# Turning q and k of the second batch by DMA instead of by TensorE, in a fused attention and mixture kernel

## The chip, the cores and the metric

The kernel runs on one core of one Trainium2 chip. The metric is device time in microseconds of one execution. Five engines run their own instruction queues in order: TensorE (PE, with its weight loads shown as PEld), VectorE (DVE), ScalarE (ACT), GpSimd (POOL) and SyncE (SP). SP and POOL also issue DMA transfers, SP through the hardware-made queue (q1 in the profile) and POOL through the software-made one (q0). All transfers are carried by the same 16 DMA engines.

## What is computed

Attention over a sliding window of 128 positions plus 4 sink positions, for 4 batches, 8 heads, 768 positions and head size 64; its output, 3072 tokens of 512 values, then goes through a mixture of 4 experts, each of two matrix products with a ReLU between, summed by normalised weights.

```python
scores = scale * np.matmul(q, k.transpose(0, 1, 3, 2))
keep = is_sink | in_window
scores = np.where(keep, scores, -1000000000.0)
a = np.exp(scores - np.max(scores, axis=-1, keepdims=True))
attn = np.matmul(a / (np.sum(a, axis=-1, keepdims=True) + 1e-09), v)
...
p = domain_probs / (domain_probs.sum(-1, keepdims=True) + 1e-09)
for e in range(E):
    h = np.maximum(x @ w1[e], 0.0)
    out += p[:, e:e + 1] * (h @ w2[e])
```

## The kernel before

**Tiles.** A batch has 6 blocks of 128 positions (`tb`), taken as 3 groups of 256 (`g`), and 4 pairs of heads (`hp`). POOL loads q and k of a block as rows, cast to bf16, into a `qkn` buffer (`load_nat`, L188; there are six such buffers), and v into `vx` (`load_v`, L253). The scores need q and k with the head dimension on the partitions: that is `qkT`, of which there is one buffer, so a batch can be turned only when the scores of the batch before are done.

**Two ways to turn.** For batches 0 and 1, `transposes` (L502) lets TensorE turn four 128x128 pieces of one group and head pair into a PSUM bank (`tr`), and ACT or DVE copies the bank to `qkT` (`copy`, L226). For batches 2 and 3, `turn_nat` (L198) issues one DMA transpose of 128x1024 elements per block on SP (L202).

**Attention** of a group and head pair: scores (L619) into two banks, exponentials on ACT (`aT`, L644), masks on DVE (L638), values (`od`, L685, with the sinks' part at L678), a reciprocal on DVE (`R`, L712), four multiplications on ACT (`onat`, L724). When the four head pairs of a group are done, SP turns `onat` into `xT` by DMA (L702), the input of the mixture. The sink keys (L543) and sink matmuls (L580) come from `qkT` too.

**Mixture.** Batch 0 goes through plain products (`hps`, L1002; `acc`, L1305). Later batches partly use products with fewer multiplications (`cps`, L1080; `acc`, L1234), whose operands DVE forms (`T`, L1054, from `xT`). While batch 1's attention runs, the mixture of batch 0 fills TensorE; while batch 2's runs, that of batch 1, and so on.

**What sets the order.** The schedule is written out by a planner in the kernel itself. It keeps a clock for each engine (`t`), charges each step by small formulas (`pe`, `act`, `dve`, `pool`, `sp`, `lands`), and at each turn of the main loop (L1363) emits the step that its books call ready, attention steps being held back until they are due against the share of mixture work done. Every engine then executes its instructions in the emitted order, with semaphores for what it waits on. Six PSUM banks (`ring`) serve all steps but the accumulators.

**Around the change.** When batch 0's attention is emitted (L1369), the gates are worked out, the remaining weights are queued on POOL, and then the rows and v of batch 1. Batch 1's attention begins with 12 `flip` steps, each one call of `transposes`, spread among its other steps. The first flip of its last group queues the rows of batch 2 on POOL and puts their six turns on the list `turns` (L820). A turn is emitted from L1380: only when the planner has its rows landed, when the earlier batch has no scores left to emit, and when no second product of batch 0 is pending (`mix.second`). After the last turn of batch 2, POOL copies two elements of `qkT` into `held` (L1384); this makes POOL wait for the turn, and the row loads of batch 3 follow it.

Of the kernel before, what the change touches and what calls it, by code (L numbers as in the profile page):

```python
# [16 lines left out]
def kernel(  # L17
# [12 lines left out]
    nc = tc.nc  # L30

    B, H, S, D = q.shape
# [12 lines left out]
    NQB = S // P  # L45
    NHP = H // 2
# [6 lines left out]
    NG = S // G  # L53
# [7 lines left out]
    START = {0: 1, 1: 1, 2: 3, 3: 3}  # L61
# [2 lines left out]
    PAIR = 1  # L64
    BEHIND = 800
    CHORES = 3
    BIASED = 1
    FAST = tuple(START)
    UNITS = ("P1", "P5", "P6", "P2", "P7", "P3", "P4")
# [5 lines left out]
    t = {"pe": 1200.0, "act": 0.0, "dve": 0.0, "pool": 1280.0, "sp": 800.0, "sw": 6500.0, "hw": 0.0}  # L75
# [20 lines left out]
    def pool(cols, *deps, fixed=190):  # L96
        at = max([t["pool"], *deps])
        t["pool"] = at + fixed + cols * 1.8
        return t["pool"] + 35
# [57 lines left out]
    landed = {}  # L157
# [147 lines left out]
    def weight_form1(e):  # L305

        w = w1_sb[e].rearrange("p (k d) (m f) -> p m k d f", k=2, m=2)
        A11, A12, A21, A22 = w[:, 0, 0], w[:, 0, 1], w[:, 1, 0], w[:, 1, 1]
        if e not in forms1:
            if START[e] < B - 1:  # L310
                x = wpool.tile([P, 3, NDB // 2, F // 2], BF16, name=f"vf_{e}", tag=f"vf_{e}")
                x = [x[:, i] for i in range(3)]
            else:
                x = [sb.tile([P, 2, H, D], BF16, name="qkn", tag="qkn", bufs=NQB) for _ in range(3)]
                x = [i.rearrange("p d h c -> p d (h c)") for i in x]
            forms1[e] = {"P1": A11, "P2": A12, "P3": x[2], "P4": A22, "P5": x[0], "P6": x[1], "P7": A21}
            formed1[e] = 0
        x = forms1[e]
        if formed1[e] == 0:
            nc.vector.tensor_add(x["P5"], A21, A22)  # L320
        elif formed1[e] == 1:
            nc.vector.tensor_sub(x["P6"], x["P5"], A11)
        elif formed1[e] == 2:
            nc.vector.tensor_sub(x["P3"], A12, x["P6"])
        else:
            nc.vector.tensor_sub(A21, A11, A21)
        formed1[e] += 1
        forms1_at[e] = dve(1024, rate=1.92)
# [3 lines left out]

    def form1_due(e):
        n = formed1.get(e, 0)
        if START[e] == B - 1 and turned_at.get((B - 1, NQB - 1), 1e12) > t["pe"]:
            return False
        return landed.get(("w1", e), 1e12) < t["pe"] and (n < 3 or n == 3 and not left1[e])

# [225 lines left out]
            run("pool")  # L564

    def turned(b, g, *hps):
        if b < 2:
            return [turned_at.get((b, g, hp), 1e12) for hp in hps or range(NHP)]
        return [turned_at.get((b, tb), 1e12) for tb in range(2 * g + 2)]

# [188 lines left out]
    class Attention:  # L759


        def __init__(self, b):
            self.b = b
            self.flips = [("transposes", b, g, hp) for g in range(NG) for hp in range(NHP)] if b < 2 else []
            self.todo, self.scored, self.valued = [], [], []
            for g in range(NG):
                if g == (1 if b == 0 else 0):
                    self.todo.append(("keys", b, 0, 0))
                self.todo += [("scores", b, hp, g) for hp in range(NHP)]
                if g and (b < ONE or g == 1):  # L770
                    self.todo.insert(2 - NHP if b == 0 else -NHP, ("sinks", b, g, 1 if b < ONE else 2))
            self.total = len(self.todo) + len(self.flips) + (1 if b else 2) * NG * NHP
            self.steps = 0
# [32 lines left out]
        def emit(self, step):  # L806
            self.steps += 1
            if step == "turn":
                turn(*self.valued.pop(0))
            elif step == "values":  # L810
                u = self.scored.pop(0)
                values(*u)
                if u[0] == 0:
                    self.valued.append(u)
                elif u[1] == NHP - 1 and u[0] + 1 < B:
                    v_loads(u[0] + 1, u[2])
            elif step == "flip":
                _, b, g, hp = self.flips.pop(0)
                transposes(b, g, hp)
                if (b, g, hp) == (1, NG - 1, 0):  # L820
                    nat_loads(2, range(NQB))
                    turns.extend((2, tb) for tb in range(NQB))
            elif step == "two":
                self.steps += 1
                for i in range(2):
                    _, b, x, y = self.todo.pop(0)
                    scores(b, x, y, i)
                    self.scored.append((b, x, y))
            else:
                kind, b, x, y = self.todo.pop(0)  # L830
                if kind == "scores":
                    scores(b, x, y)
                    self.scored.append((b, x, y))
                elif kind == "sinks":
                    sinks(b, x, y)
                elif kind == "keys":
                    sink_keys(b)
                    sink_values(b)
# [506 lines left out]
    def nat_loads(b, tbs):  # L1345
        loads.extend((load_nat, b, tb) for tb in tbs)
# [16 lines left out]
    while mix.more() or att.more():  # L1363
        now = t["pe"]

        if not att.more() and ahead == B - 1 and not wide:
            wide = 1
            mix.widened()
        if not att.more() and not loaded:  # L1369
            loaded = 1  # L1370
            gates_by_row()
            loads += [(load_w1, 3), (load_w2, 3)]
            for tb in range(NQB):
                loads.append((load_nat, 1, tb))
                if tb % 2:
                    loads += [(load_v, 1, (tb - 1,)), (load_v, 1, (tb,))]
        if loads and t["pool"] < now + 1500 and load_ready(loads[0]) < now + 1500 and free_ring(loads[0]):
            x = loads.pop(0)
            x[0](*x[1:])
        if turns and not mix.second and landed.get(("qk", *turns[0]), 1e12) < now and (turns[0][0] <= ahead or turns[0][0] == ahead + 1 and not att.todo):  # L1380
            x = turns.pop(0)
            turn_nat(*x)
            if x == (2, NQB - 1):
                nc.gpsimd.tensor_copy(out=held, in_=qkT[2][:, 1, NHP - 1, S - 2:S])  # L1384
                pool(2, turned_at[2, NQB - 1])
                nat_loads(3, range(NQB))
                turns += [(3, tb) for tb in range(NQB)]
        flush(now)
        mix.tokens()
        mix.chore()  # L1390
        if ahead:
            next_form()
        if ahead + 1 < B and not att.more() and (ahead == 0 or (ahead + 1, 0) in turned_at) and (ahead == 0 or mix.done >= sum(work[:ahead])):
            ahead += 1
            att = Attention(ahead)
            upto = mix.done
        share = (sum(work[:ahead]) - upto) * 0.96
        due = ahead == 0 or att.steps * share <= (mix.done - upto) * att.total
        opts = []
        if att.more():  # L1400
            opts = [(max(r, now), (0 if due else 3) - 0.1 * (step == "two"), "att", step) for r, step in att.options()]
        s2, p = mix.second_ready(), mix.product_ready()
        behind = max(t["dve"] - now, 0.0) + 500 * sum(x[2] == "dve" and x[0] < now + 300 for x in pend)
        opts.append((max(p, now), 1 if behind > BEHIND else 2.5, "product", None))
        opts += [(max(f, now), 2, "first", x) for f, x in mix.firsts()]
        opts.append((max(s2, now), 1 if mix.since >= 1 else 2.5, "second", None))
        soonest = min(o[0] for o in opts)
        if soonest > now + 40 and flush(soonest, True):
            continue
        if soonest < 20000 and soonest > now + 220:  # L1410
            idle_products(acc[1], 1, G)
            continue
        if soonest > 1e11:
            if loads:
                x = loads.pop(0)
                x[0](*x[1:])
            else:
                turn_nat(*turns.pop(0))
            continue
        r, _, kind, step = min(opts, key=lambda o: (o[0] > now + 40, o[0] if o[0] > now + 40 else 0, o[1]))  # L1420
        assert r < 1e11
        if kind == "att":
            att.emit(step)
        elif kind == "first":
            mix.emit_first(step, r)
        elif kind == "product":
            mix.emit_product()
        else:
            mix.emit_second()
# [36 lines left out]
```

The softmax here doesn't subtract the row's maximum and nothing guards it: scores larger than these inputs give would overflow.

## Time and profile before

| | us |
|---|---|
| median of 4 runs | 372.28 (372.0 to 372.53) |
| the profiled execution | 372.0, of which the profile's span is 370.3 |

| group of instructions | count | mean ns | busy us |
|---|---|---|---|
| PE transposes, `tr` (L513) | 96 | 219 | 7.8 |
| ACT read-outs of 512 columns, `qkT` from `tr` (L226) | 14 | 594 | 7.7 |
| DVE read-outs of 512 columns, `qkT` from `tr` (L226) | 6 | 422 | 2.4 |
| SP issue of a DMA transpose of `qkn` (L202) | 12 | 1282 (median) | |
| ACT multiplications, `onat` (L724) | 144 | 325 | 33.3 |

The span is the profiled execution as its instruction records show it; the time of the run is somewhat longer. "Busy" of a group adds the durations with overlaps taken out. A matmul's duration is the time that it spends in TensorE's pipeline, and consecutive ones overlap, so the pace of a series is read from its start and the start of what follows. The software queue's packets took 51.8% of the 16 DMA engines' span, the hardware queue's 21.5%. The granted TensorE clock was 0.999.

### The profile page before, as it was taken

The page shows a single profiled execution, that of the slowest core. Times are in us where ns is not written, and L with a number is a line of the kernel's source. Part 1 is how long each engine was busy: PE and PEld are TensorE (multiplying, and loading weights), DVE is VectorE, ACT ScalarE, POOL GpSimd, SP SyncE. Part 2 cuts the span into 40 slices and gives each one's busy share as a digit, 9 for nine tenths or more (in the row PEclk, how much of TensorE's full clock was granted, in tenths as well). Part 3 has the DMA queues.
Part 4 walks back from the last instruction along what each step waited for, and adds up shares of the span by engine and source line. Part 5 has one row for each costly group of instructions (what it writes and reads, how often), then busy time and mean ns, then how long its engine had stood idle before and what let it go on. Part 6 is the DMA issues. An engine that isn't in the chain of part 4 may idle for free.

```text
span 370.3 us, 9961 instructions
## 1 busy us (share of the span) xinstructions
PE 361.0 (97%) x4167; PEld 299.5 (81%) x4167; DVE 287.2 (78%) x636; ACT 157.6 (43%) x402; POOL 71.3 (19%) x91
## 2 busy tenths in 40 slices
PE   6899999999999999999999999999999999999996
PEld 2585766667767788898888898899999999999985
DVE  5674997674554799779969979869898988899860
ACT  4764723685665245446435445552103213222110
POOL 8935113708040192010020000000000000000000
PEclk9999999999999999999999999999999999999999
DMA  9999999949999999519692041215002111020011
GB/s 164 165 189 198 210 212 180 155 30 107 150 126 206 166 120 112 74 57 88 113 165 81 13 104 30 44 44 87 16 19 84 30 43 58 16 73 2 2 58 57
DMA packets 110952, 35.63 MB, mean 96 GB/s; under 512 B 94276, under 2 KB 106404, under 8 KB 110908
## 3 DMA queue, kind: packets, MB, share of 16 engines
q0 software_dynamic: 77520, 17.31, 51.8%
q1 hardware_dynamic: 32332, 17.18, 21.5%
q8 instruction: 32, 0.52, 0.6%
q10 hardware_dynamic: 1056, 0.52, 0.5%
q14 instruction: 12, 0.10, 0.1%
HBM read 40.45 MB, written 6.34 MB: 126 GB/s over the span
## 4 chain that ended last, share of the span: by engine, by line
PE 87%; DVE 6%; DMA 3%; ACT 2%; issue 1%; ACTq 0%; DVEq 0%
PE acc L1234 29%; PE hps L1002 20%; PE cps L1080 19%; PE acc L1305 9%; PE sps L619 3%; PE od L685 2%; DMA xT<-onat 2%; DMA kraw<-in_k_dram 2%; PE tr L513 1%; ACT aT L644 1%; PE od L678 1%; DVE H L1026 1%; DVE aT L638 1%; DVE onat L715 1%; PE tx L743 1%
## 5 line engine op out<-in xcount | busy, mean ns | idle before, releaser
L1002 PE MATMUL hps<-xT,w 128*128 128x256 bf16 x768 | 95.6, 273 | 0.1
L1002 PEld LDWEIGHTS <-w 128*128 128x128 bf16 x768 | 72.3, 98 | 12.2 <-issue 2.6
L1234 PEld LDWEIGHTS <-H 128*128 128x128 bf16 x600 | 56.0, 98 | 6.4 <-issue 0.8
L644 ACT ACTIVATE aT<-sps 128x512 bf16<-128x512 f32 (+1 forms) x96 | 47.2, 571 | 30.6 <-PE sps L619 30.6
L1080 PEld LDWEIGHTS <-w 128*128 128x128 bf16 x768 | 48.2, 98 | 2.0 <-issue 0.5
L1234 PE MATMUL acc<-w,H 128*128 128x256 bf16 x360 | 48.0, 273 | 0.0
L724 ACT ACTIVATE onat<-od,R 128x64 bf16<-128x64 f32 x144 | 33.3, 325 | 34.0 <-DVE R L712 32.1
L1305 PE MATMUL acc<-w,H 128*128 128x512 bf16 x192 | 45.4, 379 | 0.0
L1099 DVE SCALAR_TENSOR_TENSOR H<-cps,gates 128x512 bf16<-128x512 f32 x57 | 38.7, 684 | 2.1 <-PE cps L1080 1.2
L1277 ACT COPY osb<-acc 128x256 f32<-128x256 f32 x36 | 13.5, 375 | 58.4 <-PE acc L1234 55.7
L1026 DVE SCALAR_TENSOR_TENSOR H<-hps,gates 128x512 bf16<-128x512 f32 x44 | 30.0, 686 | 9.3 <-PE hps L1002 9.1
L255 POOL DMA_DIRECT2D vx<-in_v_dram x24 | 21.3, 896 | 74.6 <-PE od L685 65.9
L1305 PEld LDWEIGHTS <-H 128*128 128x128 bf16 x192 | 18.3, 98 | 17.5
L1234 PE MATMUL acc<-wf,H 128*128 128x256 bf16 x240 | 31.9, 273 | 0.0
L1015 ACT ACTIVATE H<-hps 128x512 bf16<-128x512 f32 x36 | 21.5, 598 | 23.9 <-PE hps L1002 23.6
L1234 PEld LDWEIGHTS <-S 128*128 128x128 bf16 x288 | 27.0, 98 | 3.3 <-issue 0.5
L1080 PE MATMUL cps<-T,w 128*128 128x128 bf16 x384 | 29.3, 219 | 0.0
L1080 PE MATMUL cps<-xT,w 128*128 128x128 bf16 x384 | 29.1, 219 | 0.0
L1108 ACT COPY cps<-cps 128x512 f32<-128x512 f32 x24 | 13.8, 575 | 33.1 <-PE cps L1080 31.0
L1080 PEld LDWEIGHTS <-vf 128*128 128x128 bf16 x432 | 26.9, 98 | 1.0 <-issue 0.3
L1317 DVE SCALAR_TENSOR_TENSOR osb<-acc,scale_t,osb 128x512 f32<-128x512 f32 x18 | 13.5, 749 | 15.6 <-PE acc L1305 15.6
L190 POOL DMA_DIRECT2D qkn<-in_q_dram x22 | 19.8, 899 | 18.2 <-PE tr L513 9.0
(116 smaller groups left out, 532.3 us busy)
## 6 DMA issues: line engine op xcount, KB each, us to landing
w<-in_moe_w_dram POOLq DMA_DIRECT2D x7, 1024.0 KB, 18.9
out_dram<-osb SPq DMA_DIRECT2D x23, 256.0 KB
gates<-gate_rows SPq DMA_DIRECT2D x36, 128.0 KB
vx<-in_v_dram POOLq DMA_DIRECT2D x24, 128.0 KB, 6.4
qkn<-in_q_dram POOLq DMA_DIRECT2D x22, 128.0 KB, 6.8
qkn<-in_k_dram POOLq DMA_DIRECT2D x22, 128.0 KB, 7.0
w<-in_moe_w_dram POOLq DMA_DIRECT2D x2, 512.0 KB, 8.5
kraw<-in_k_dram ACTq DMA_DIRECT2D x2, 256.0 KB
```

The costliest lines, as they stand in the source:

```text
L190: nc.gpsimd.dma_start(out=both[:, i], in_=src[b, :, tb * P:(tb + 1) * P, :].rearrange("h p d -> p h d"),)
L255: nc.gpsimd.dma_start(out=vx[tb][:, :, 0:D], in_=v[b, :, tb * P:(tb + 1) * P, :].rearrange("h p d -> p h d"),)
L644: nc.scalar.activation(out=a[:, ph], in_=sps[ph][:, 0:w], func=AF.Exp, scale=scale)
L724: nc.scalar.mul(o[:, qi, hp, ph * D:(ph + 1) * D], od[:, qi, ph, 0:D], R[:, qi, ph])
L1002: nc.tensor.matmul(h[:, i].rearrange("p (q n) -> p q n", q=2), lhsT=w1_sb[e][:, db, fb * P:(fb + 1) * P], rhs=xT[b, g][:, :, db], start=(i ...
L1015: nc.scalar.activation(out=dst, in_=h, func=AF.Relu)
L1026: nc.vector.scalar_tensor_tensor(out=dst, in0=h, scalar=0.0, in1=gate, op0=ALU.max, op1=ALU.mult,)
L1080: nc.tensor.matmul(y[:, f], lhsT=A[:, d, f * P:(f + 1) * P], rhs=T[:, d], start=(m in ("P1", "P5") and f == 0 and d == 0), stop=(d == 1), ...
L1099: nc.vector.scalar_tensor_tensor(out=dst, in0=src, scalar=0.0, in1=gate, op0=ALU.max, op1=ALU.mult)
L1108: nc.scalar.copy(out=tiles["Y"], in_=y)
L1234: nc.tensor.matmul(x, lhsT=self.operand(b, g, e, m)[:, f], rhs=forms[e][m][:, f], start=(k == 0 and f == 0 and m in (("P1", "P5", "P2") if ...
L1305: nc.tensor.matmul(op, lhsT=H[:, fb // QF, fb % QF, s], rhs=w2_sb[e][:, fb, :], start=(fb == 0), stop=(fb == NFB - 1),)
```

## The change

Batch 1's rows are turned by six DMA transposes on SP, by `turn_nat`, as in batches 2 and 3. The flips of batch 1 are gone; what they did besides, queueing batch 2's rows and turns, moves to the emission of batch 1's last turn, and this place now also makes the `held` copy for batch 1 as it did for batch 2. While batch 0 or batch 1 is the batch in attention, turns are no longer held back by `mix.second`. Scores of batch 1 wait for whole blocks (`turned`). The test for which experts borrow `qkn` buffers for their formed weights is written as `e < OWN`; with `OWN = 2` it gives the same experts as the old test.

```diff
--- before.py
+++ after.py
@@ -64,6 +64,7 @@
     PAIR = 1
     BEHIND = 800
     CHORES = 3
+    OWN = 2
     BIASED = 1
     FAST = tuple(START)
     UNITS = ("P1", "P5", "P6", "P2", "P7", "P3", "P4")
@@ -307,7 +308,7 @@
         w = w1_sb[e].rearrange("p (k d) (m f) -> p m k d f", k=2, m=2)
         A11, A12, A21, A22 = w[:, 0, 0], w[:, 0, 1], w[:, 1, 0], w[:, 1, 1]
         if e not in forms1:
-            if START[e] < B - 1:
+            if e < OWN:
                 x = wpool.tile([P, 3, NDB // 2, F // 2], BF16, name=f"vf_{e}", tag=f"vf_{e}")
                 x = [x[:, i] for i in range(3)]
             else:
@@ -332,7 +333,7 @@
 
     def form1_due(e):
         n = formed1.get(e, 0)
-        if START[e] == B - 1 and turned_at.get((B - 1, NQB - 1), 1e12) > t["pe"]:
+        if e >= OWN and turned_at.get((B - 1, NQB - 1), 1e12) > t["pe"]:
             return False
         return landed.get(("w1", e), 1e12) < t["pe"] and (n < 3 or n == 3 and not left1[e])
 
@@ -564,7 +565,7 @@
             run("pool")
 
     def turned(b, g, *hps):
-        if b < 2:
+        if not b:
             return [turned_at.get((b, g, hp), 1e12) for hp in hps or range(NHP)]
         return [turned_at.get((b, tb), 1e12) for tb in range(2 * g + 2)]
 
@@ -761,7 +762,7 @@
 
         def __init__(self, b):
             self.b = b
-            self.flips = [("transposes", b, g, hp) for g in range(NG) for hp in range(NHP)] if b < 2 else []
+            self.flips = [("transposes", b, g, hp) for g in range(NG) for hp in range(NHP)] if not b else []
             self.todo, self.scored, self.valued = [], [], []
             for g in range(NG):
                 if g == (1 if b == 0 else 0):
@@ -817,9 +818,6 @@
             elif step == "flip":
                 _, b, g, hp = self.flips.pop(0)
                 transposes(b, g, hp)
-                if (b, g, hp) == (1, NG - 1, 0):
-                    nat_loads(2, range(NQB))
-                    turns.extend((2, tb) for tb in range(NQB))
             elif step == "two":
                 self.steps += 1
                 for i in range(2):
@@ -1370,6 +1368,7 @@
             loaded = 1
             gates_by_row()
             loads += [(load_w1, 3), (load_w2, 3)]
+            turns += [(1, tb) for tb in range(NQB)]
             for tb in range(NQB):
                 loads.append((load_nat, 1, tb))
                 if tb % 2:
@@ -1377,14 +1376,15 @@
         if loads and t["pool"] < now + 1500 and load_ready(loads[0]) < now + 1500 and free_ring(loads[0]):
             x = loads.pop(0)
             x[0](*x[1:])
-        if turns and not mix.second and landed.get(("qk", *turns[0]), 1e12) < now and (turns[0][0] <= ahead or turns[0][0] == ahead + 1 and not att.todo):
+        if turns and (ahead < 2 or not mix.second) and landed.get(("qk", *turns[0]), 1e12) < now and (turns[0][0] <= ahead or turns[0][0] == ahead + 1 and not att.todo):
             x = turns.pop(0)
             turn_nat(*x)
-            if x == (2, NQB - 1):
-                nc.gpsimd.tensor_copy(out=held, in_=qkT[2][:, 1, NHP - 1, S - 2:S])
-                pool(2, turned_at[2, NQB - 1])
-                nat_loads(3, range(NQB))
-                turns += [(3, tb) for tb in range(NQB)]
+            b = x[0]
+            if 0 < b < B - 1 and x[1] == NQB - 1:
+                nc.gpsimd.tensor_copy(out=held, in_=qkT[b][:, 1, NHP - 1, S - 2:S])
+                pool(2, turned_at[x])
+                nat_loads(b + 1, range(NQB))
+                turns += [(b + 1, tb) for tb in range(NQB)]
         flush(now)
         mix.tokens()
         mix.chore()
```

In the instruction streams of the two programs TensorE's order is the same up to the first transposes of batch 1 and again from the first product of the mixture with `cps` (L1080) to the end. On SP the six new transposes stand between the two writes of `gate_rows` and the first transpose of `onat`. On POOL the rows of batch 2 follow the new `held` copy in one series of twelve loads, and v blocks 3 to 5 of batch 2 come behind the rows of batch 3, where they stood ahead of them.

## The prediction

> **What bounds the kernel now.** I read the page's header and busy times first, then the busy time by stretches, then the chain of waits from 60 to 112 us, where the second batch's transposes lie, then the queues that the new transfers join.
>
> ```profile
> span 370.3 us, 9961 instructions
> PE 361.0 (97%) x4167; PEld 299.5 (81%) x4167; DVE 287.2 (78%) x636; ACT 157.6 (43%) x402; POOL 71.3 (19%) x91
> ...
> 60.00:68.00 8.00, 8.00 (x55) 5.14 (x54) 6.00 (x9) 2.68 (x5) 5.13 (x6) 1.00 2.37 157
> 68.00:80.00 12.00, 11.72 (x126) 7.95 (x124) 8.72 (x22) 9.83 (x29) 4.50 (x6) 1.00 1.58 100
> 80.00:90.00 10.00, 10.00 (x107) 7.19 (x106) 5.89 (x12) 5.85 (x20) 5.95 (x7) 1.00 0.70 59
> ```
>
> Each stretch row gives its length, then the busy us of PE, PEld, DVE, ACT and POOL with counts, the granted clock, the DMA share (summed queue time, so it can pass 1) and GB/s. PE is busy 361.0 of 370.3 us at full clock; outside the first 20 us and the last 4 it hardly idles. So the time is TensorE's own work: what leaves PE shortens the kernel, what leaves ACT or DVE does so only where PE waits for it. The same rows show the danger: from 60 to 77 us the DMA engines are full (2.37).
>
> **Removed from PE.** A count of each engine's instructions in the two programs gives 48 of the 96 L513 transposes gone and no other matmul added or lost. Their price is in the chain (start, us, what):
>
> ```profile
> 68.33 0.89 PE tr L513 x16
> 69.23 0.87 PE hps L1002 x8
> ...
> 72.67 1.53 PE tr L513 x16
> 74.20 0.88 PE hps L1002 x8
> ```
>
> The first sixteen take 0.89 us, 55.6 ns each; the page's 219 ns is a duration in the pipeline, not a pitch. 48 x 55.6 ns = **2.67 us**. The second sixteen follow 0.24 us of waiting for ACT, and 1.37 us pass until the next matmul (72.67 to 74.04 in the timeline), 0.48 above the price: 0.72 us of stall that goes with them.
>
> Here a rule differs. The Trainium skill ("TensorE: Matmul & The Clock Gate", Part 4: PE-mode transpose) gives about 275 ns for a 128x128 bf16 transpose in one kernel: 48 x 275 ns = 13.2 us, a kernel of about 359 us. The trace says 55.6 ns, because the transposes stand back to back; I take the trace.
>
> **Removed from ACT and DVE.** Twelve read-outs of 512 columns (L226): 8 on ACT at 594 ns (4.8 us), 4 on DVE at 422 ns (1.7 us). Three H read-outs move from DVE (L1017, 689 ns) to ACT (L1015, 598 ns). Both engines have PE's work as cover here; gain beyond the stall above: nothing. Uncovered, 6.5 us could not all count, since PE idles only 0.38 us from 68 to 100.
>
> **Added: six turns on SP.** The program puts them after the gate rows (sent at 46.6 us) and before the first xT transpose (85.54). SP issues nothing between 48.3 and 85.5, so 6 x 1.28 us of issuing (L202, median) is free. When they run is set by the row loads on POOL's queue:
>
> ```profile
> 32.45 0.88 POOL L190 DMA_DIRECT2D qkn<-in_k_dram  x1
> ...
> 42.46 0.88 POOL L190 DMA_DIRECT2D qkn<-in_k_dram  x1 [4.29 <-DMA w<-in_moe_w_dram]
> ...
> 64.24 0.88 POOL L190 DMA_DIRECT2D qkn<-in_k_dram  x1
> ...
> 69.85 0.90 POOL L190 DMA_DIRECT2D qkn<-in_k_dram  x1
> ```
>
> These are the last loads of row blocks 0, 1, 3 and 5. With the issue-to-landing times of the DMA view (31.5, 23.3, 7.0, 6.4 us) the rows are in at 64.0, 65.8, 71.2 and 76.3.
>
> A turn beside row loads: the nearest case is the xT transpose of the same 128x1024 elements.
>
> ```profile
> 85.54 6.41 DMA xT<-onat
> ```
>
> It is issued about 2 us before its packets run. They run from 87 to 91 us, some 1066 in all. In the microsecond from 89 the two queues stood like this (packets, MB, share of 16 engines):
>
> ```profile
> q0 software_dynamic: 555, 0.07, 125.0%
> q1 hardware_dynamic: 419, 0.11, 66.1%
> ```
>
> So a turn among row loads gets some 420 packets/us: 2.5 us of moving, and the row loads, at about 1228 packets/us when alone, lose about 1.3 us to it. This is also what the skill warns of ("DMA: Bandwidth & Descriptors", Rules for kernel authors): another issuing engine gives no more bandwidth, all feed the same 16 DMA engines and interleave. If SP's queue were free of POOL's, the six turns would end 2.5 us (the uncontended turn at 177.7 us) after their rows, by 79; with the trace's sharing: block 0 at 68.5, block 1 at 71; block 3's rows slip 3.9 us to 75.1 and turn by 79.6; block 5's slip 6.5 to 82.8 and turn by 87.3.
>
> When does PE ask? Up to 68.17 its order is unchanged. Then come 40 L1002 and 24 L1305 matmuls (0.87 and 1.73 us for eight): 9.55 us, first scores of batch 1 at **77.7** (blocks 0, 1; slack 6.7). Adding the pieces in order, the sinks matmul that reads blocks 2 and 3 stands at **82.1** (slack 2.5) and the last group's scores at **89.1** (slack 1.8). Cost on PE: nothing in the likeliest case. Bounds: 0, and, with 6.41 us for every turn one after the other, block 3 at 89.6 and block 5 at 102.4, 7.5 + 5.8 us of stall. I take 0, being nearest to the packet rates.
>
> On DVE, the sink keys (L543) wait for turn 0 and stand behind the second L1305 read-out after 74 us: covered. What xT waits for is moved by little: issued near 86 again, again among batch 2's rows, so DVE waits there as now (2.25 us before L1054, at the price of about 0.2 us on PE).
>
> **Moved.** The attention of batch 1 starts 6 us later (77.7 against 71.8) and ends no later, so it is packed more tightly, and ACT carries it:
>
> ```profile
> 72.13 2.40 ACT L644 ACTIVATE aT<-sps 128x384 bf16<-128x384 f32 x6 [1.34 <-PE sps L619]
> ...
> 80.77 2.07 ACT L644 ACTIVATE aT<-sps 128x512 bf16<-128x512 f32 x4 [0.58 <-PE sps L619]
> 84.59 1.85 ACT L724 ACTIVATE onat<-od,R 128x64 bf16<-128x64 f32 x8 [1.76 <-DVE R L712]
> ```
>
> Paces: 0.40 us per L644 of 384 columns, 0.52 of 512, 0.93 per four L724. In the new order, from the first exponential to those of the last group's first half: 8 x 0.40 + 12 x 0.52 + 2 x 0.4 (sinks) + 6 x 0.93 = 15.8 us, 78 to 94, without a gap, while the kernel's own book counts four L724 at 0.51. PE wants the last of these masked by about 95, so it fits narrowly; single waits for a bank or an aT are likely. Bounds 0 to 2.5 us (six times 0.42 us of under-counting); I take **0.6**, near the 0.72 of the same kind of stall now.
>
> The marker copy on POOL (L1384) now runs twice. The first waits for turn 5 (87), then come batch 2's rows, all twelve at once; now they start at 84.9 and the last four wait 9.0 us for L513, until 100.9. They are in by about 103, and their turns wait for the last scores anyway. The second marker comes some 15 us earlier than at present (129.6). Behind it are batch 3's rows and only then v blocks 3 to 5 of batch 2, issued about 127 instead of 119.5, wanted after 140: hidden. From the first L1080 matmul on, PE's order is the same to the end, so a lead gained by 103 us stays.
>
> **Sum**, against the profiled execution (372.0 us, span 370.3): 372.0 - 2.67 - 0.72 + 0.6 = 369.2. The median is 0.28 above that run: **369.5 us**. For this kernel 0.2% (0.75 us) is what can be told from no change.
>
> **Rivals.**
> 1. ACT is the bound in the packed stretch, 2.5 us of stall (above): 371.4 us. For it: the tally without a gap. Against: PE's mixture work can run ahead of attention.
> 2. Turns are late, the kernel slower. Place: the sinks matmul at 82.1. It decides once the first four turns, from 64.0, need over 4.5 us each. At 5.5 us: block 3 at 86.0 (3.9 us stall), block 5 at 97.0 (4.0 more): 372.3 - 2.8 + 7.9 = 377.4 us. For it: the 6.41 row, and the fullest DMA stretch. Against: that row includes 2 us of start that overlaps the turn before, and the packet rates.
> 3. The skill's 275 ns: 359 us; against it, the 0.89 us row.
> 4. It does not do what it says: excluded by the counts (48 transposes, 18 turns).
>
> **Numbers.** Forecast 0.68 (own range 368.6 to 370.6); rival 1 0.18, of which half stays within 0.2%; rival 2 0.12; rival 3 0.02. The range to 372.3 takes in rival 1 and the edge of rival 2. Faster 0.77 (forecast, rival 3, some of rival 1), same 0.09, slower 0.14.
>
> **What would show it.** Right: 48 tr rows; first scores near 77.7 with no wait for a DMA; first L1080 at 116.6 instead of 119.4; the same lead at the end; PE idle no larger. Wrong: PE waiting for qkT by DMA at the sinks or last scores, ACT without a gap and PE waiting for aT beyond 1 us in 78 to 96, or the lead at 116 lost later to batch 3's rows.

## The result, and the profile after

| | before | changed |
|---|---|---|
| median, us | 372.04 (60 runs) | 370.65 (40 runs) |
| ratio to before, 95% interval | | 0.9968, 0.9960 to 0.9977 |
| the profiled execution, us | 372.0 | 369.71 |
| its span, us | 370.3 | 368.0 |

The kernel is faster by 0.32% (0.23 to 0.40%), some 1.2 us (the two medians alone differ by 1.4). The forecast was 369.5 us, 2.8 us below the median of the four runs that it had, 372.28: the right direction, but by the ratio less than half of the forecast gain came. Line numbers of the changed kernel differ by one or two: L513 is now L514 (transposes), L580 L581 (sinks), L619 L620 (scores), L1002 L1000, L1305 L1303, L1080 L1078.

The page of the changed kernel: PE's share of the span is higher, its work 1.7 us less.

```profile
span 368.0 us, 9878 instructions
PE 359.3 (98%) x4119; PEld 298.2 (81%) x4119; DVE 282.9 (77%) x629; ACT 154.4 (42%) x397; POOL 71.4 (19%) x92
```

The timeline of PE tells more (start, us, engine, line, what, count; in brackets the idle time before it and what the profile thinks ended it):

```profile
77.16 0.67 PE L620 MATMUL sps<-qkT 64*128 64x256 bf16 x12
78.08 1.03 PE L1000 MATMUL hps<-xT,w 128*128 128x256 bf16 x8 [0.24 <-ACT aT L645]
...
82.60 0.29 PE L581 MATMUL sinks<-qkT,ksd 128*32 128x256 bf16 x4 [0.72 <-ACT onat L725]
...
86.39 0.53 PE L620 MATMUL sps<-qkT 64*128 64x128 bf16 x6
88.05 0.29 PE L581 MATMUL sinks<-qkT,ksd 128*32 128x256 bf16 x4 [1.14 <-ACT aT L645]
...
117.45 0.61 PE L1078 MATMUL cps<-xT,w 128*128 128x128 bf16 x8
```

Two holes have come, both ahead of a sinks matmul: 0.72 and 1.14 us. The kernel before had none at these places; its first `cps` matmul started at 119.23 us and its last matmul ended at 366.83, here at 117.45 and 364.89. So the lead is 1.8 us at 117 and 1.9 at the end. But 0.65 us of it was there before the programs differ (the L1000 group that follows the last common one starts at 67.52, where the transposes before started at 68.17), which is chance between two executions. The stretch itself gave 1.1 us, near the 1.2 us of the ratio. The account of it: 2.67 us of transposes and the 0.48 us of stretching are gone, the 0.24 us wait for ACT has stayed (78.08), the holes took 0.72 and 1.14: 3.15 - 1.86 = 1.29 us.

**Who made the holes?** The bracket says ACT. The weight loads say otherwise. The `sinks` weights (`ksd`) need nothing of ACT; their instruction waits for two DMA transfers, the turns of blocks 2 and 3 at the first and of 4 and 5 at the second. PEld's timeline:

```profile
77.76 0.10 PEld L1000 LDWEIGHTS <-w 128*128 128x128 bf16 x1 [0.16 <-issue]
78.08 0.75 PEld L1000 LDWEIGHTS <-w 128*128 128x128 bf16 x7 [0.22 <-issue]
...
82.57 0.13 PEld L581 LDWEIGHTS <-ksd 128*32 128x32 bf16 x4 [0.81 <-issue]
...
88.02 0.13 PEld L581 LDWEIGHTS <-ksd 128*32 128x32 bf16 x4 [1.33 <-issue]
```

At 78.08, where the matmul really waits for ACT, its weights went in 0.32 us ahead of it. At 82.57 and 88.02 the weights come only 0.03 us ahead of the matmul, so the weight load itself was held. And POOL, whose marker copy waits for nothing but the turn of block 5, started at the same moment:

```profile
87.97 0.19 POOL L1384 COPY held<-qkT 128x2 bf16<-128x2 bf16 x1 [12.81 <-DMA qkT<-qkn]
```

The semaphore record of the trace has the landings themselves: the turns of blocks 0 to 5 were in at 72.5, 76.2, 78.9, 82.5, 85.6 and 87.9 us, those of blocks 3 and 5 each 0.1 us ahead of the weight load that waited for them.

This is a reading of one execution, with two theories left standing: **the turn theory** (the sinks matmuls wait for late turns) and **the ACT theory** (the crowded ACT gives banks back late: the forecast's first rival, for which it had set aside 0.6 us). The experiments tell them apart.

### The profile page after: what moved, and what is told of

Same layout as the page of the kernel before. It is cut to its first block, busy times and chain, and to the rows that moved or that the text cites. A ratio compares the mean times of both kernels' runs of the same rounds, so it can differ in the third digit from the quotient of the medians.

```text
span 368.0 us, 9878 instructions
## 1 busy us (share of the span) xinstructions
PE 359.3 (98%) x4119; PEld 298.2 (81%) x4119; DVE 282.9 (77%) x629; ACT 154.4 (42%) x397; POOL 71.4 (19%) x92
## 3 DMA queue, kind: packets, MB, share of 16 engines
q10 hardware_dynamic: 1056, 0.52, 0.5%
## 4 chain that ended last, share of the span: by engine, by line
PE 86%; DVE 4%; DMA 3%; ACT 3%; POOL 2%; issue 1%; POOLq 0%; ACTq 0%; DVEq 0%
PE acc L1232 29%; PE hps L1000 21%; PE cps L1078 20%; PE acc L1303 10%; DMA w<-in_moe_w_dram 3%; PE od L686 2%; PE sps L620 2%; ACT aT L645 1%; ACT onat L725 1%; POOL qkn L191 1%; PE od L679 1%; DVE H L1024 1%; POOL vx L256 1%; DVE aT L639 1%; DVE H L1097 0%
## 5 line engine op out<-in xcount | busy, mean ns | idle before, releaser
L1000 PE MATMUL hps<-xT,w 128*128 128x256 bf16 x768 | 95.0, 273 | 0.9 <-DMA w<-in_moe_w_dram 0.5
L1000 PEld LDWEIGHTS <-w 128*128 128x128 bf16 x768 | 72.9, 98 | 13.9 <-issue 1.6
L1078 PEld LDWEIGHTS <-w 128*128 128x128 bf16 x768 | 48.3, 98 | 2.0 <-issue 0.5
L1303 PE MATMUL acc<-w,H 128*128 128x512 bf16 x192 | 45.4, 379 | 0.0
L1013 ACT ACTIVATE H<-hps 128x512 bf16<-128x512 f32 x39 | 23.2, 599 | 35.7 <-PE hps L1000 35.4
L1303 PEld LDWEIGHTS <-H 128*128 128x128 bf16 x192 | 18.1, 98 | 17.9 <-issue 0.3
L1078 PE MATMUL cps<-T,w 128*128 128x128 bf16 x384 | 29.3, 219 | 0.0
L1078 PE MATMUL cps<-xT,w 128*128 128x128 bf16 x384 | 29.1, 219 | 0.0
L1078 PEld LDWEIGHTS <-vf 128*128 128x128 bf16 x432 | 26.9, 98 | 1.0 <-issue 0.3
L639 DVE TENSOR_TENSOR aT<-aT,mask 128x1024 bf16<-128x1024 bf16 (+1 forms) x36 | 22.7, 639 | 5.2 <-ACT aT L645 5.2
```

Of the source, the lines that this page charges most:

```text
L639: nc.vector.tensor_mul(a, a, m[:, None, :].to_broadcast([P, 2, w]))
L1000: nc.tensor.matmul(h[:, i].rearrange("p (q n) -> p q n", q=2), lhsT=w1_sb[e][:, db, fb * P:(fb + 1) * P], rhs=xT[b, g][:, :, db], start=(i ...
L1013: nc.scalar.activation(out=dst, in_=h, func=AF.Relu)
L1078: nc.tensor.matmul(y[:, f], lhsT=A[:, d, f * P:(f + 1) * P], rhs=T[:, d], start=(m in ("P1", "P5") and f == 0 and d == 0), stop=(d == 1), ...
L1303: nc.tensor.matmul(op, lhsT=H[:, fb // QF, fb % QF, s], rhs=w2_sb[e][:, fb, :], start=(fb == 0), stop=(fb == NFB - 1),)
```

## The experiments

Each was compared with the kernel before on the same chip; the ratio to compare with is the changed kernel's 0.9968. The edits are to the changed kernel unless said otherwise.

**1. Lighter ACT** (`act_light`).

```diff
+                if b == 1:
+                    nc.scalar.copy(out=o[:, :, hp].rearrange("p q (h d) -> p q h d", h=2), in_=od[:, :, :, 0:D])
                 for qi in range(2):
                     for ph in range(2):
-                        nc.scalar.mul(o[:, qi, hp, ph * D:(ph + 1) * D], od[:, qi, ph, 0:D], R[:, qi, ph])
+                        b == 1 or nc.scalar.mul(o[:, qi, hp, ph * D:(ph + 1) * D], od[:, qi, ph, 0:D], R[:, qi, ph])
```

> In batch 1 the four scaling multiplications on ACT for a group and head pair become one plain copy of 256 columns (the division by the sum of the exponentials is left out in batch 1); orders otherwise as in the changed kernel. It frees ACT of some 0.5 us for each of 12. ACT theory: both holes close, ratio 0.991 to 0.992. Turn theory: they stay, at most the 0.24 us wait at 78 us goes, ratio 0.995 to 0.997.

Measured: 370.09 us, ratio 0.9956 (0.9937 to 0.9975): no gain that can be told from the changed kernel. In its PE timeline the holes stay (the first is shorter, because PE comes to it 0.7 us later in this execution), and with ACT out of the way the profile names the turn:

```profile
82.98 0.29 PE L581 MATMUL sinks<-qkT,ksd 128*32 128x256 bf16 x4 [0.36 <-DMA qkT<-qkn]
...
88.23 0.29 PE L581 MATMUL sinks<-qkT,ksd 128*32 128x256 bf16 x4 [1.07 <-DMA qkT<-qkn]
```

The ACT theory falls.

**2. Turns with less beside them** (`no_v1`).

```diff
-            nc.gpsimd.dma_start(
+            b == 1 or nc.gpsimd.dma_start(
                 out=vx[tb][:, :, 0:D],
...
```

> The six v loads of batch 1 are left out (batch 1's values use the v of batch 0), with the order of PE, DVE, ACT and SP as in the changed kernel; this takes a third of POOL's packets out of the stretch in which the turns run. Turn theory: the turns of blocks 3 and 5 land 3 to 4 us earlier, ahead of the two sinks matmuls, both holes close, ratio 0.991 to 0.992. ACT theory: ACT's work is the same, the holes stay, ratio 0.996 to 0.997.

Measured: 369.12 us, ratio 0.9922 (0.9904 to 0.9941). The marker copy on POOL runs at 80.96 instead of 87.97, and PE's timeline has the sinks without a wait:

```profile
82.49 0.29 PE L581 MATMUL sinks<-qkT,ksd 128*32 128x256 bf16 x4
...
87.13 0.29 PE L581 MATMUL sinks<-qkT,ksd 128*32 128x256 bf16 x4
```

With the turns in time the kernel gains 2.9 us on the before of the same chip, about the 2.8 that the forecast had summed. The turn theory holds. ACT is not far behind, though: this timeline has one wait of 0.48 us for it, at 91.51, which the changed kernel has not.

**3. One turn twice** (`turn5_twice`).

```diff
+        if (b, tb) == (1, NQB - 1):
+            nc.sync.dma_start(
+                out=qkT[b][:, :, :, tb * P:(tb + 1) * P].rearrange("c i h p -> c (i h) p"),
+                in_=nat[b, tb].rearrange("p i h d -> p (i h d)"), transpose=True,
+            )
         turned_at[b, tb] = sp(
...
```

> The turn of block 5 of batch 1 is issued twice (the same data), all other orders as in the changed kernel. Turn theory: the second sinks matmul waits for the second copy, 3.5 to 4 us later than now, ratio 1.006 to 1.007. ACT theory: the turn is in by 86 us (its last packets) with 2 us to spare, so half of the shift is hidden, ratio 1.000 to 1.002.

Measured: 375.10 us, ratio 1.0087 (1.0068 to 1.0106), more than either theory's number. PE's timeline, second sinks matmul and what follows:

```profile
92.45 0.29 PE L586 MATMUL sinks<-qkT,ksd 128*32 128x256 bf16 x4 [4.24 <-DMA qkT<-qkn]
92.68 3.41 PE L1308 MATMUL acc<-w,H 128*128 128x512 bf16 x8
```

The wait is 3.1 us longer than the changed kernel's 1.14, and eight L1308 matmuls then take 3.41 us, where they took 1.90: PE's clock had dropped (last section). The two together, 4.6 us, are about the 4.5 us between the medians of this kernel and the changed one. This also puts a size on the forecast's second rival: a turn about 4 us later, with the drop of the clock that follows, does make the kernel slower than before.

**4. The price of the transposes** (`flips_twice`, an edit to the kernel before).

```diff
-                nc.tensor.transpose(tr[:, i, tt], rows, ident)
+                for _ in range(2 if b == 1 else 1):
+                    nc.tensor.transpose(tr[:, i, tt], rows, ident)
```

> The kernel before, with each of the 48 TensorE transposes of batch 1 issued twice in a row into the same place (the same result). By the trace's pitch of 55.6 ns: 2.67 us more, ratio 1.006 to 1.009. By some 275 ns each: 13.2 us more, ratio 1.035. If they were hidden under waits: 1.000 to 1.003.

Measured: 373.98 us, ratio 1.0059 (1.0045 to 1.0073): 2.2 us (1.7 to 2.7), 46 ns each. Part of the second series fits into stretching that was there anyway:

```profile
68.29 1.95 PE L514 MATMUL tr<-ident,qkn 128*128 128x128 bf16 x32
...
73.69 1.95 PE L514 MATMUL tr<-ident,qkn 128*128 128x128 bf16 x32 [0.24 <-DMA qkn<-in_q_dram]
```

Thirty-two take 1.95 us in both places, though sixteen took 1.53 at 72.67 before: 2.67 - 0.48 = 2.19. The forecast's price of 2.67 us lies at the edge of the interval and stands; 275 ns each does not.

**5. Other order of the loads** (`rows_first`): blocks 0 to 3 of q and k, v of 0 and 1, blocks 4 and 5, the rest of v.

```diff
-            for tb in range(NQB):
-                loads.append((load_nat, 1, tb))
-                if tb % 2:
-                    loads += [(load_v, 1, (tb - 1,)), (load_v, 1, (tb,))]
+            loads += [(load_nat, 1, tb) for tb in range(4)] + [(load_v, 1, (tb,)) for tb in range(2)]
+            loads += [(load_nat, 1, tb) for tb in (4, 5)] + [(load_v, 1, (tb,)) for tb in range(2, NQB)]
```

> Of batch 1's loads on POOL, blocks 0 to 3 of q and k come first, then v of blocks 0 and 1, then q and k of blocks 4 and 5, then the rest of v; PE, DVE, ACT and SP keep the order of the changed kernel. Turn theory: the turns of blocks 3 and 5 land about 2 us earlier, the two holes (0.8 and 1.1 us) close or nearly so, unless v of blocks 0 and 1, now later, is missed by the first values at 79 us; ratio 0.991 to 0.993. Against it: the sum of all rows is the same, so the gain is no more than 0.5 us, ratio 0.996.

Measured: 372.29 us, ratio 1.0011 (0.9993 to 1.0028). A miss: the marker copy runs at 89.77, so the last turn is later, not earlier. The rows of block 3 were in 4.2 us earlier (69.6 instead of 73.8), but its turn landed at 83.3, no earlier than the 82.5 of the changed kernel: it stood behind the turns ahead of it. The rows of block 5 came at 83.0 as before, and its turn took until 89.7 instead of 87.9. The v loads that were moved back now run beside the last turns. Queue packets in the microsecond from 85 (packets, MB, share of 16 engines), first here and then in the changed kernel from 84:

```profile
q1 hardware_dynamic: 487, 0.12, 84.2%
q0 software_dynamic: 380, 0.05, 72.1%
```

```profile
q1 hardware_dynamic: 905, 0.22, 103.0%
q0 software_dynamic: 5, 0.00, 0.9%
```

In this kernel, then, loads that PE doesn't wait for are better ahead of the last turns than beside them. The holes of 0.99 and 2.07 us were followed by a drop of the clock here too.

**6. Books put later.** The planner emits a sinks matmul as soon as its books say that the turns are in; by the trace they were not yet, and the turn of block 5 was 1.1 us later than PE. Three kernels add nothing but time to the planner's books for batch 1: `book_late` 3.5 us to all turns, `late_both` the same and 4 us to the `xT` transposes, `late23_both` 3.5 us to the turns of blocks 2 to 5 and 4 us to `xT`. The edit of the last:

```diff
-        turned_at[b, tb] = sp(landed["qk", b, tb], scored_at.get(b - 1, 0.0), issue=1330, takes=1400) + LATE
+        turned_at[b, tb] = sp(landed["qk", b, tb], scored_at.get(b - 1, 0.0), issue=1330, takes=1400) + LATE + (3500 if b == 1 and tb > 1 else 0)
...
-                turned_out = sp(at, issue=1330, takes=1400)
+                turned_out = sp(at, issue=1330, takes=1400) + (4000 if b == 1 else 0)
```

> The planner's book for when a turn of batch 1 is ready is put 3.5 us later; no instruction is added or removed, but TensorE's order then has more mixture work ahead of the scores and the sinks matmuls of batch 1. Turn theory (the 0.82 and 1.15 us holes ahead of the two sinks matmuls are waits for the turns of blocks 3 and 5): both holes go, about 368.8 us where the changed kernel has 370.65, ratio to before 0.991 to 0.992. ACT theory (they are waits for banks and aT that the crowded ACT gives back late): attention is packed as tightly as in the changed kernel, holes of 1.5 us or more stay, ratio 0.996 to 0.997.

Measured: 369.77 us, ratio 0.9944 (0.9925 to 0.9964). Half of what was expected. Both holes are gone, but a new one came, first in PE's timeline, then what lies behind it in DVE's:

```profile
111.80 1.07 PE L1303 MATMUL acc<-w,H 128*128 128x512 bf16 x4 [1.66 <-DVE H L1015]
```

```profile
109.39 0.29 DVE L1052 TENSOR_TENSOR T<-xT 128x256 bf16<-128x256 bf16 x1 [4.66 <-DMA xT<-onat]
...
111.06 0.69 DVE L1015 TENSOR_SCALAR H<-hps 128x512 bf16<-128x512 f32 x1
```

DVE stood 4.66 us at an operation of no urgency, waiting for `xT` (issued at 100.28, behind batch 2's row loads), with the H read-out that PE needed queued behind it.

> As the kernel with all turns of batch 1 booked 3.5 us later, and its xT transposes booked 4 us later too. If the 1.66 us hole at 110 us came from DVE reaching T (which waits for xT) too early, it closes: ratio 0.990 to 0.992, from 0.9944. If the hole came from ACT or from a bank, it stays: 0.994.

Measured: 368.28 us, ratio 0.9910 (0.9895 to 0.9924); no hole at 110.

> The planner's book is put later by 3.5 us for the turns of blocks 2 to 5 of batch 1 and by 4 us for its xT transposes; no instruction more or less. If late books are all that was wrong: no hole ahead of the sinks matmuls, and none near 110 us where the kernel with only the turns booked later lost 1.7 us to DVE waiting for xT; ratio 0.991 to 0.993. If waits only move on to another place: 0.994 or more.

Measured: 368.07 us, ratio 0.9902 (0.9885 to 0.9918), the fastest of all: 3.6 us under before. Its PE timeline:

```profile
77.06 0.67 PE L620 MATMUL sps<-qkT 64*128 64x256 bf16 x12 [0.28 <-DMA qkT<-qkn]
...
86.20 0.29 PE L581 MATMUL sinks<-qkT,ksd 128*32 128x256 bf16 x4
...
90.55 0.29 PE L581 MATMUL sinks<-qkT,ksd 128*32 128x256 bf16 x4
...
115.08 0.61 PE L1078 MATMUL cps<-xT,w 128*128 128x128 bf16 x8
```

The second sinks matmul stands at 90.55 with no wait; in this kernel the turn of block 5 was in by 88.6. The same mixture work fills the time ahead of it.

**7. Is it the `xT` book alone?** The last line of that edit by itself, in the changed kernel (`xt_late`) and in the kernel before (`before_xt_late`).

> The changed kernel with only the xT transposes of batch 1 booked 4 us later; TensorE's order is the changed kernel's, DVE's moves in eight places. Turn theory: both holes ahead of the sinks matmuls stay, ratio 0.994 to 0.997. If the late xT were what the changed kernel lost to: 0.991 or less.

Measured: 371.14 us, ratio 0.9986 (0.9968 to 1.0003). No better than the changed kernel; the expected range was missed on the slow side. Both holes stay (1.62 and 1.16 us), and the first scores wait 0.61 us for a turn. Five of the twelve executions have a mean clock of 0.995 or less and a median of 372.2 us, the other seven 370.8 (last section).

> The kernel before with its xT transposes of batch 1 booked 4 us later; it tells how much of the gain of the kernel with both books put later belongs to the turning by DMA at all. DVE waited 2.25 and 0.88 us for xT in the kernel before, at a price of some 0.2 us on PE: ratio 0.998 to 1.001. If it gains 0.5% or more, the kernel before would have had half of the repair without the change.

Measured: 371.53 us, ratio 0.9991 (0.9979 to 1.0003). So the gain of `late23_both` is not the `xT` book's: it needs the turning by DMA, booked where the turns really land, and the `xT` book only keeps the wait from coming back at 110 us.

## Why the prediction was wrong

**The step that failed: "the last group's scores at 89.1 (slack 1.8). Cost on PE: nothing in the likeliest case."** It named the wrong reader. Blocks 4 and 5 are first read by the second sinks matmul of batch 1, which stands right after the scores at 86.39 and 3.3 us ahead of the last group's scores:

```profile
88.05 0.29 PE L581 MATMUL sinks<-qkT,ksd 128*32 128x256 bf16 x4 [1.14 <-ACT aT L645]
...
91.34 0.62 PE L620 MATMUL sps<-qkT 64*128 64x128 bf16 x12
```

Taken 3.3 us ahead of the forecast's 89.1 it stood at 85.8, so that block 5's turn, at the forecast's own 87.3, left a hole of 1.5 us there. Measured, the turn was in at 87.9, and PE would have been ready at 86.2 (it was at 86.9, after the first hole of 0.72). So this one instruction accounts for the whole 1.86 us: PE has no idle time between the two sinks matmuls, so without the first hole the second would have been longer by as much. The term that the forecast put at nothing was 1.86 us. With the 0.24 us of stall that stayed, and without the 0.6 us for ACT, the sum is 372.0 - 2.67 - 0.48 + 1.86 = 370.7 us; the median is 370.65.

**The turn of block 3 was mis-sized**: 82.5 instead of 79.6, and it began with block 0, in at 72.5 instead of 68.5. The rows came as worked out. The DMA view of the changed kernel gives issue to landing for the last loads of blocks 3 and 5 (issued 63.95 and 69.52):

```profile
qkn<-in_k_dram POOLq DMA_DIRECT2D x1, 128.0 KB, 9.8
...
qkn<-in_k_dram POOLq DMA_DIRECT2D x1, 128.0 KB, 13.5
```

So they were in at 73.8 and 83.0; the forecast had 75.1 and 82.8. What was wrong is the rate of a turn beside row loads, 420 packets/us, read from one microsecond of one transfer. Over the 16 us from 66 to 82 the queues moved

```profile
q0 software_dynamic: 9645, 1.22, 143.3%
q1 hardware_dynamic: 4224, 1.05, 60.3%
```

4224 packets are four whole turns of 1056: 4.0 us each, pauses between them included, instead of 2.5. So the turns queued up. Block 3's rows were in at 73.8, but the first packet of its turn ran at 79.0, behind the turn of block 2; its own packets then took 2.9 us. `rows_first` shows the same: earlier rows, no earlier turn. The forecast held 6.41 us and 2.5 us as the ends and chose the lower end outright; the packet rates pointed there, but from a sample too short.

**The ACT term (0.6 us) did not come.** The tally of 15.8 us without a gap cost nothing here: making ACT lighter gained nothing (experiment 1).

**What held:** PE's own work as the bound; the price of the transposes (2.67 us; a doubling gave 2.2, 1.7 to 2.7); 0.48 of the 0.72 us of stall gone, the other 0.24 kept; no sign of a gain from the read-outs taken off ACT and DVE (1.29 us worked out without one, 1.1 found in the stretch); the lead at 117 us kept to the end, with batch 3's rows and the late v loads hidden. That the first scores stood at 77.2 (forecast 77.7) without a wait for DMA was partly luck: the turn of block 1 was in 1.0 us ahead of them, not 6.7, and in `xt_late`, with TensorE's order unchanged, they waited 0.61 us. The second rival had the right mechanism and the right place. Its sign, more than 4.5 us for each of the first four turns from 64.0, was met: they took 18.5 us, 4.6 each. Its price of 7.9 us was worked out for 5.5 us each; the holes measured 1.9.

## What to carry to other kernels

Moving work from a full engine to a queue gains its price only where each reader of the moved result still finds it ready: list every reader in program order, small side instructions first, before giving a slack. Where a planner sets the order, the gain is in its books: with the landings of the turns booked 3.5 us later and those of `xT` 4 us, the same work gave 1.0% instead of 0.3%. And a wait that the profile puts down to one engine is checked at the weight load or at another waiter of the same transfer, before that engine is blamed.

## What the runs showed of the hardware

**Turns and row loads together are slower than either alone.** Row loads alone moved some 1228 packets/us, a turn with little beside it 905 (at 84 us). In the microsecond from 69 of the changed kernel the two moved

```profile
q1 hardware_dynamic: 340, 0.09, 100.1%
q0 software_dynamic: 246, 0.03, 90.4%
```

586 packets in all, with queue shares near full. Over the whole stretch from 66 to 82 it was 867 per us. At the two rates that each had alone, the packets of that stretch (9645 and 4224) would have needed an estimated 7.85 + 4.67 = 12.5 us instead of 16. An equal interleaving of the two, which the forecast assumed, does not explain that; what does was not tried. The issue on SP stretched as well: 3.4 us for the turns of blocks 1 and 2, against 1.28 (median) in the kernel before.

**A hole of 2 us can cost more than 2 us.** In `rows_first` the 2.07 us hole ended at 89.85. Its trace has half of the clock from 89.77 to 93.18. The stretches around it, columns as in the prediction (the clock is the last but two):

```profile
86.36:89.77 3.41, 1.42 (x23) 0.82 (x22) 2.57 (x5) 3.41 (x11) 0.00 (x1) 1.00 1.13 111
89.77:93.18 3.41, 3.33 (x12) 1.21 (x13) 0.69 (x1) 1.10 (x6) 3.11 (x5) 0.50 0.74 189
93.18:96.59 3.41, 3.30 (x43) 2.63 (x42) 1.93 (x5) 2.13 (x7) 3.41 (x5) 1.00 1.92 145
```

The granted clock was half for 3.41 us, and the eight L1303 matmuls after the hole took 3.36 us instead of 1.90. The Trainium skill ("TensorE: Matmul & The Clock Gate", Why this matters for your kernels) warns of idle gaps over some 3 us; here 2.07 us, after a hole of 0.99 six us earlier, was enough.

The traces hint at what decides. From the first moment of full clock, the stretches of one clock are whole numbers of steps of 3.413 us, up to the last change at the end of the kernel: 25 steps full, one at half and 82 full here, 26, 1 and 81 in `turn5_twice`. The steps ahead of the two drops had PE busy for 1.42 and 0.45 us. Steps with 1.70 us busy (`book_late`, 108.60 to 112.01, around its hole of 1.66 us), 1.79 (`xt_late`) and 2.27 (the changed kernel, 85.79 to 89.20) were followed by no drop. So what counts seems to be how much of one step is idle, with the limit, in these traces, between 1.42 and 1.70 us of work. Where the steps begin differs from one execution to the next (7.28 us in the changed kernel, 4.44 in `rows_first`), so the same hole may fall into one step or two. This was not tried with a run of its own.

The drop does not come each time: of the twelve executions of `rows_first`, seven have a mean clock of 0.995 and a median of 372.9 us, five a clock of 1.0 and 371.5 us. The changed kernel, with a 1.1 us hole in its profile, has such a clock (0.995 or less) in seven of some forty executions; `late23_both` in none of five.
